# New assumed costs, a due time one pair sooner and a fourth row buffer in the planner of an attention and MLP kernel

## The chip, the cores and the metric

The kernel runs on one core of a Trainium2 chip. The metric is the device time of one execution in microseconds (us), and the median of several runs is compared. The engines are called as in the profile: PE (TensorE matmul), PEld (its weight loads), DVE (VectorE), ACT (ScalarE), POOL (GpSimd) and SP (SyncE, which here issues all DMAs).

## The reference, cut to what matters

```python
# attention: q, k, v are (8, 8, 576, 64), float32
scores = np.matmul(q, k.transpose(0, 1, 3, 2)) / np.sqrt(64)
scores = np.where(block_i >= block_j, scores, -1e9)     # blocks of 64, causal by block
attn = np.exp(scores - scores.max(-1, keepdims=True))
attn = attn / (attn.sum(-1, keepdims=True) + 1e-09)
o = np.matmul(attn, v)                                  # heads joined: x is (8, 576, 512)
# layer norm and MLP with a residual
mu, var = mean(x), mean((x - mu) ** 2)
xn = (x - mu) / np.sqrt(var + 1e-06) * g_ln
return x + np.maximum(xn @ w_ch1, 0.0) @ w_ch2          # 512 -> 2048 -> 512
```

The weights come in as 64-bit numbers; the kernel decodes them to float32 itself.

## The kernel before, in words

**Work.** Attention goes over 32 pairs of heads (`pair(k)`). For a pair, PE makes scores (L416), DVE takes the row minimum of the negated scores while it masks them (`soften`, L434), ACT takes the exponential (L437), PE transposes (L446), ACT or DVE copies the transposed block out of PSUM (`evac`, L234 for ACT and L236 for DVE), PE multiplies with v (L452, L456), and DVE transposes the result (L530). On PE the transposes and products of pair k stand behind the scores of pair k + 1. Every eighth pair, `first(m)` handles the first 64 positions of eight pairs (L568 to L615 on PE, DVE, ACT and POOL).

The MLP handles 36 tiles of 128 rows in rounds of 8, 8, 8, 8 and 4 tiles. A round has 8 weight groups; each makes 7 products (L867, a one-level Strassen scheme on operands split into a high and a low part) and then the second matrix product (L927), whose results DVE adds up (L936). Before a round, `norm_tiles(n, q)` normalises its rows two tiles at a time (four calls in a round of eight; `x0` buffers in round 0, `x` buffers in later rounds), and `operands(n)` makes the sums, differences and high and low parts (`diff` L754, `split` L763 and L765, tile `xm`). `decode(j, second)` decodes 32 pieces of the weights: ACT (L350, L355), POOL (L353, L373), DVE (L359, L362), and a cast on ACT or DVE. In round 0, `stream` turns decoded pieces into group operands (L818 loads `wf`, L826 sums on POOL, L837 low parts, L845 stores).

**Order.** The order of all instructions is written by a planner (`Plan.run`), which plays the program with assumed costs: `add(engine, cost, ...)` gives each task an assumed time, `any_of` lets the planner choose between engines by which would finish first, and a ready task with the lowest `prio` goes first on its engine. The order of instructions on each engine, and the engine of each `any_of` task, is then fixed; the chip runs each engine's list in that order, with waits. The assumed times change nothing else in the program.

**Priorities.** A pair k has `prio` 100 + 10 k and a little more at each step. So a task with `prio` 100 + 10 c stands behind the pairs before c and ahead of the pairs after c: it is a filler until pair c and overtakes from then on. `norm_tiles` of round 0 has c = 10 + 3 q + LATER, the operands of round 0 c = 22 + LATER, and decoding piece n has c = 12 + 0.97 n + LATER. `first(m)` has c = 8 m + 3. The MLP's own tasks have `prio` 0 to 4 for what follows a product. A task also has a gate, an earlier event that it waits for, which the change leaves alone. A rule in the planner (`AHEAD`) holds back a filler on DVE or ACT if a task of a pair at least half a pair more urgent will be ready before the filler's assumed end less 0.25 us.

**Buffers.** Tiles share pools: `small` has 21 tiles of 128x512, with a limit for each kind (`ya` 10, `x` 3, `t` 4, `tt` 4, `mag`, `sgn`, `xnt`, `x0`, `sum` 2 and others).

Of the kernel before, what the change touches and what calls it, by code (L numbers as in the profile page):

```python
# [9 lines left out]
F32 = mybir.dt.float32  # L10
# [8 lines left out]
P = 128  # L19
# [8 lines left out]
TILES = sum(ROUNDS)  # L28
D_0, D_1 = 12.0, .97
LN_0, LN_1 = 10, 3  # L30
LATER = 3
AHEAD = 100, 5, .25


# [155 lines left out]
def dve(n):  # L190
    return .07 + n / 960


def act(n, sbuf=False):
    return .055 + .085 * sbuf + n / 1200


def pool(n):
    return .07 + n / 440

@with_exitstack
def attn_mlp_kernel(ctx: ExitStack, tc: tile.TileContext, qk, qk0, v, v0, w1, w2, g, out):
# [8 lines left out]
    nc = tc.nc  # L211
# [16 lines left out]
    def any_of(fn, **costs):  # L228

        return {e: (c, lambda e=e: fn(engines[e])) for e, c in costs.items()}  # L230
# [51 lines left out]
    def small(name, shape, dtype, most):  # L282
        return kind(name, shape, dtype, 21, None, "small", most)
# [8 lines left out]
    new_ot, new_v0 = small("ot", [P, 512], F32, 2), small("v0", [P, 512], F32, 1)  # L292
    new_e0, new_pt00, new_ot0 = (small(n, [P, 512], F32, 1) for n in ("e0", "pt00", "ot0"))
    new_mag, new_sgn = (small(n, [P, 512], I32, 2) for n in ("mag", "sgn"))
    new_ya, new_x, new_xnt = (small(n, [P, 512], F32, k) for n, k in (("ya", 10), ("x", 3), ("xnt", 2)))
    new_x0, new_xn = small("x0", [P, 512], F32, 2), small("xn", [P, 512], F32, 1)
    new_t, new_tt, new_sum = small("t", [P, 512], F32, 4), small("tt", [P, 2, 2, P], F32, 4), small("sum", [P, 2, 256], F32, 2)
    xs = [kind(f"xm{p}", [P, max(ROUNDS) // 2, 2, 2, P], F32R, 1)() for p in range(7)]
# [37 lines left out]
    def decode(j, second, prio, gate):  # L336
# [6 lines left out]
        def dma():  # L343
# [12 lines left out]
            out=sgn(), in_=wv(0).bitcast(U32), func=AF.Copy, scale=2.0 ** -29 * (1 - 2.0 ** -9), bias=-0.499),  # L356
            r=[word], w=[sign], prio=prio)
        sign2 = Buf(parent=sgnb)
        add("DVE", dve(n), lambda: nc.vector.scalar_tensor_tensor(  # L359
            out=sgn(), in0=wv(1), scalar=-2147483648, in1=sgn(), op0=ALU.bitwise_and, op1=ALU.bitwise_or),  # L360
            r=[sign, word], w=[sign2], prio=prio)
        add("DVE", dve(n), lambda: nc.vector.scalar_tensor_tensor(  # L362
            out=sgn(), in0=mag(), scalar=3, in1=sgn(), op0=ALU.logical_shift_left, op1=ALU.bitwise_or),
            r=[sign2, mag2], w=[full], prio=prio)
        w = lambda: sgn().bitcast(F32)
# [180 lines left out]
    def first(m):  # L546
# [4 lines left out]
        def pr():  # L551
            step[0] += 1
            return prio + .05 * step[0]
# [31 lines left out]
        def total():  # L585
            nc.vector.tensor_reduce(out=nm.t, in_=ev(e.t), op=ALU.add, axis=AX.X)
            nc.vector.tensor_scalar_add(nm.t, nm.t, 1e-9)
            nc.vector.reciprocal(nm.t, nm.t)
        add("DVE", dve(512) + .4, total, r=[p, *d], w=[r1], prio=pr())
        add("POOL", pool(512), lambda: nc.gpsimd.tensor_mul(  # L590
            ev(e.t), ev(e.t), nm.t.unsqueeze(2).to_broadcast([P, 8, 64])), r=[p, r1], w=[pn], prio=pr())
        tr, pt, turned_ = new_tr(), new_pt00(), Buf()
# [49 lines left out]
    def norm_tiles(n, q, prio, gate):  # L642
# [74 lines left out]
        for h, (x, part) in enumerate(rows):  # L717
            unit, scaled = Buf(parent=x), Buf(parent=x)
            if n:
                add("ACT", act(512, True), lambda x=x, h=h: nc.scalar.activation(  # L720
                    out=x.t, in_=x.t, func=AF.Identity, bias=norm.t[:, 10 + h:11 + h], scale=norm.t[:, 4 + h:5 + h]),
                    r=[rstd], w=[unit, *part], prio=prio)
            else:
                add("DVE", dve(512), lambda x=x, h=h: nc.vector.tensor_scalar(  # L724
                    out=x.t, in0=x.t, scalar1=norm.t[:, 2 * h:2 * h + 1], scalar2=norm.t[:, 4 + h:5 + h],
                    op0=ALU.subtract, op1=ALU.mult), r=[rstd], w=[unit, *part], prio=prio)
            add(any_of(lambda e, x=x: e.tensor_mul(x.t, x.t, g_sb), POOL=pool(512)), r=[unit, gb], w=[scaled], prio=prio)
            xnt, xw = new_xnt(), new_xw()
            add("DVE", dve(512), lambda x=x, xnt=xnt: nc.vector.transpose(xnt.t, x.t), r=[scaled], w=[xnt], prio=prio)
            parts = []  # L730
            for g4 in range(4):
                parts.append(Buf(parent=xw))
                load(32 * 2048, lambda xw=xw, xnt=xnt, g4=g4: nc.sync.dma_start(
                    out=xw.t[:, 32 * g4:32 * g4 + 32].rearrange("(k r) q -> r k q", r=32),
                    in_=xnt.t[32 * g4:32 * g4 + 32].rearrange("p (k q) -> p k q", q=32)), r=[xnt], w=[parts[-1]], prio=prio)
            half = Buf(parent=xt)
            load(P * 2048, lambda xw=xw, h=h: nc.sync.dma_start(
                out=xt.t[:, h].rearrange("p (c q) -> p c q", q=P), in_=xw.t.rearrange("(c p) q -> p c q", p=P)),
                r=parts, w=[half], alloc=[xt], prio=prio)
            ready.append(half)  # L740
# [4 lines left out]
    def operands(n, prio):  # L745
# [5 lines left out]

        def diff(p, q, i, in0, in1, r, w):
            new = Buf(parent=tts[q])
            add(any_of(lambda e: e.tensor_sub(tmp(q, i), in0(), in1()), DVE=dve(256), POOL=pool(256)),  # L754
                r=r, w=[new, *w], prio=prio + .1 * p + .01 * q)
            return new

        def split(step, p, q, src, r):
            old = held.get((n - 1, p), [])
            hi, lo = Buf(parent=xs[p]), Buf(parent=xs[p])  # L760
            three = lambda x: x.rearrange("p (c n) -> p c n", c=2)
            pr = prio + .1 * step + .01 * q
            add(any_of(lambda e: copy(e, xs[p].t[:, q, 0], three(src())), ACT=act(256, True), DVE=.08 + 256 / 1920),  # L763
                r=r, w=[hi, *old], prio=pr)
            add(any_of(lambda e: e.tensor_sub(xs[p].t[:, q, 1], three(src()), xs[p].t[:, q, 0]),  # L765
                       DVE=dve(256), POOL=pool(256)), r=[hi, *r], w=[lo, *old], prio=pr)
            got.setdefault(p, []).extend((hi, lo))
            return hi, lo

# [242 lines left out]
```

## Time and profile before

| | us |
|---|---|
| median of 3 runs | 1050.07 |
| lowest and highest run | 1049.4, 1050.23 |
| the profiled execution's own time | 1050.46 |
| its span, first to last instruction | 1048.7 |
| PE busy in the span | 1037.1 |

The profile is of one execution. Busy time of PE has modelled ends, so that small waits inside a stretch of matmuls may count as busy; the starts of instructions are the better ruler. An instruction's time in the trace may overlap the one behind it on the same engine a little.

### The profile page before, as it was taken

To read this page: it belongs to the slowest core of one execution; us is meant where nothing else is said; L and a number is where in the kernel's file an instruction comes from. 1 tells how busy PE (TensorE), PEld (TensorE's weight loads), DVE (VectorE), ACT (ScalarE), POOL (GpSimd) and SP (SyncE) were. 2 spreads that over 40 slices of the span, in tenths; PEclk is the share of its full clock that TensorE was granted. 3 is DMA by queue.
4 is the path that set the end of the run, shared out by engine and by line. 5 is a ranking of instruction groups with operands and counts; after the bars stand their busy time and mean duration, and the time that the engine had idled before them with its cause. 6 is when DMAs were issued, how large, how long until landed. Compare 5 with 4: busy or idle time off the path is not lost.

```text
span 1048.7 us, 17977 instructions
## 1 busy us (share of the span) xinstructions
PE 1037.1 (99%) x6256; PEld 852.4 (81%) x6256; DVE 743.7 (71%) x1629; ACT 524.0 (50%) x1264; POOL 286.3 (27%) x468
## 2 busy tenths in 40 slices
PE   8999999999999999999999999999999999999998
PEld 7877777777878888888888888888888888888997
DVE  5778999989878878885656684665595555465544
ACT  6999888899875535342433341343242322122221
POOL 0223454545343765340222240222240220000000
PEclk9999999999999999999999999999999999999999
DMA  7578889898779898858777647688657667336873
GB/s 270 200 256 266 222 288 279 234 300 295 261 272 306 276 310 238 251 209 265 217 243 213 231 159 259 186 242 248 183 200 262 207 192 251 139 111 249 299 279 126
DMA packets 237930, 248.91 MB, mean 237 GB/s; under 512 B 159376, under 2 KB 188048, under 8 KB 227600
## 3 DMA queue, kind: packets, MB, share of 16 engines
q1 hardware_dynamic: 237840, 247.77, 72.9%
q8 instruction: 49, 0.80, 0.3%
q14 instruction: 41, 0.34, 0.1%
HBM read 182.71 MB, written 65.01 MB: 236 GB/s over the span
## 4 chain that ended last, share of the span: by engine, by line
PE 90%; DVE 7%; DMA 1%; issue 1%; ACT 0%; SPq 0%; POOL 0%; DVEq 0%; POOLq 0%; ACTq 0%
PE y L927 36%; PE p L867 32%; PE tr L446 7%; PE s L416 7%; PE o L456 5%; PE o L452 2%; DVE pab L434 1%; DMA wc<-wcs 1%; DVE pu L434 1%; DMA x<-xd 1%; DVE sgn L359 0%; DVE x L724 0%; DVE ya L936 0%; DVE xm L765 0%; PE tr L326 0%
## 5 line engine op out<-in xcount | busy, mean ns | idle before, releaser
L927 PE MATMUL y<-wc,h 128*128 128x512 f32 x1728 | 433.8, 390 | 0.2 <-DVE h L887 0.2
L927 PEld LDWEIGHTS y<-wc,h 128*128 128x128 f32 x1728 | 322.1, 188 | 66.4 <-DVE h L887 1.3
L936 DVE TENSOR_TENSOR ya<-y,ya 128x512 f32<-128x512 f32 x288 | 197.6, 687 | 181.6 <-PE y L927 178.8
L867 PE MATMUL p<-xm,wa 128*128 128x512 f32 (+1 forms) x960 | 221.7, 368 | 0.0
L867 PEld LDWEIGHTS p<-xm,wa 128*128 128x128 f32 x960 | 169.9, 188 | 31.5 <-issue 0.2
L867 PE MATMUL p<-xm,wb 128*128 128x512 f32 (+1 forms) x720 | 166.2, 368 | 0.0
L875 ACT COPY t<-p 128x512 f32<-128x512 f32 (+1 forms) x120 | 65.2, 544 | 167.8 <-PE p L867 166.0
L867 PEld LDWEIGHTS p<-xm,wb 128*128 128x128 f32 x720 | 127.7, 188 | 23.7
L886 ACT ACTIVATE h<-t 128x512 fp32r<-128x512 f32 (+1 forms) x120 | 62.2, 579 | 162.5 <-DVE t L880 162.3
L880 DVE TENSOR_TENSOR t<-p,t 128x512 f32<-128x512 f32 (+1 forms) x120 | 76.3, 636 | 47.9 <-PE p L867 43.2
L416 PE MATMUL s<-raw 64*128 64x224 f32 (+3 forms) x768 | 97.2, 388 | 2.5 <-DVE nm L434 2.0
L437 ACT ACTIVATE pab<-pab,nm 128x448 f32<-128x448 f32 (+1 forms) x128 | 91.2, 731 | 0.2 <-DVE nm L434 0.2
L234 ACT COPY pt<-tr 128x512 f32<-128x512 f32 x166 | 87.0, 597 | 7.2 <-PE tr L446 5.8
L416 PEld LDWEIGHTS s<-raw 64*128 64x128 f32 x768 | 74.8, 188 | 18.8 <-issue 5.1
L434 DVE CUSTOM_DVE_ANT_0 pab<-s,never 128x448 f32<-128x448 f32 (+1 forms) x128 | 82.7, 684 | 2.2 <-PE s L416 1.8
L456 PE MATMUL o<-pt,v 128*64 128x256 f32 (+1 forms) x768 | 80.1, 344 | 0.0
L456 PEld LDWEIGHTS o<-pt,v 128*64 128x64 f32 x768 | 55.3, 137 | 27.6
L887 DVE SCALAR_TENSOR_TENSOR h<-t,h 128x512 fp32r<-128x512 f32 (+1 forms) x120 | 74.1, 666 | 3.9 <-ACT h L886 3.8
L353 POOL TENSOR_SCALAR mag<-mag 128x512 f32<-128x512 f32 x32 | 48.7, 1525 | 101.4 <-ACT mag L350 92.4
L681 POOL TENSOR_SCALAR norm<-norm 128x1 f32<-128x1 f32 x28 | 6.9, 245 | 248.5 <-ACT xn L678 248.5
L437 ACT ACTIVATE pu<-pu,nm 128x320 f32<-128x320 f32 (+1 forms) x128 | 64.8, 510 | 19.5 <-DVE nm L434 18.5
L446 PE MATMUL tr<-ident,pab 128*128 128x128 f32 x512 | 63.3, 274 | 3.9 <-DVE nm L434 2.8
(96 smaller groups left out, 1036.3 us busy)
## 6 DMA issues: line engine op xcount, KB each, us to landing
wc<-wcs SPq DMA_DIRECT2D x40, 1024.0 KB, 7.0
wa<-was SPq DMA_DIRECT2D x32, 1024.0 KB, 6.3
wb<-wbs SPq DMA_DIRECT2D x32, 768.0 KB, 5.8
raw<-qk SPq DMA_DIRECT2D x32, 576.0 KB, 4.8
wr<-w SPq DMA_DIRECT2D x32, 512.0 KB, 6.1
v<-v SPq DMA_DIRECT2D x32, 320.0 KB, 5.5
x<-xd SPq DMA_DIRECT2D x144, 64.0 KB, 3.9
xrow<-x SPq DMA_DIRECT2D x36, 256.0 KB, 3.9
```

The source lines that it names most:

```text
L234: e.copy(out=out, in_=in_)
L416: nc.tensor.matmul(x, raw.t[HALF[h], 0, col], raw.t[HALF[h], 1, at:at + x.shape[1]], start=True, stop=True)
L434: add("DVE", dve(n) + .01, lambda: nc.vector.tensor_tensor_reduce(out=two(p.t[:, part(i, h)]), in0=mine(), in1=two(hide), scale=-0.125, sc ...
L437: add("ACT", act(n, True) + .14, lambda: nc.scalar.activation(out=p.t[:, part(i, h)], in_=p.t[:, part(i, h)], func=AF.Exp, bias=nm.t[:, at ...
L446: nc.tensor.transpose(o.t[:, n * P:(n + 1) * P], x, ident)
L456: nc.tensor.matmul(o.t[HALF[h], at + lo:at + 256], v_sb.t[:, ck, HALF[h]], rhs(h), start=False, stop=(n == len(steps) - 1), skip_group_che ...
L867: nc.tensor.matmul(x.t[:, 0:TN], w_(l), xs[m].t[:, 0:half, o, k], start=start and k == e == 0, stop=k == 1 and e == 2, skip_group_check=True)
L875: add("ACT", act(TN), lambda: nc.scalar.copy(out=t.t[:, 0:TN], in_=x.t[:, 0:TN]), r=[r], w=[new], prio=0)
L880: add("DVE", dve(TN), lambda: nc.vector.tensor_add(t.t[:, 0:TN], x.t[:, 0:TN], t.t[:, 0:TN]), r=r, w=[new], prio=0)
L887: add("DVE", dve(TN), lambda: nc.vector.scalar_tensor_tensor(out=x.t[:, 1, 0:TN], in0=src(), scalar=0.0, in1=x.t[:, 0, 0:TN], op0=ALU.max, ...
L927: nc.tensor.matmul(yb.t, x.t[:, l, at:at + P], wc.t[:, i, o], start=i == e == 0, stop=i == 1 and e == 2)
L936: add("DVE", dve(512), lambda yb=yb, ya=ya: nc.vector.tensor_add(ya.t, yb.t, ya.t), r=[part, before_], w=[now], prio=1)
```

## The change

Assumed times of some tasks become longer: two DVE instructions of decoding and one of normalisation (`dve2`), the differences and low parts of `operands` on DVE (`dve2`), its casts on DVE (`cast`), all POOL tasks priced by `pool`, and the sum in `first` on DVE (0.4 us more). `LATER` goes from 3 to 2. The kind `x` (rows of rounds 1 to 4) may have four buffers of the pool `small`, which stays at 21.

```diff
-LATER = 3
+LATER = 2
 def pool(n):
-    return .07 + n / 440
+    return .1 + n / 390
+def dve2(n):
+    return .1 + n / 760
+def cast(n):
+    return .2 + n / 1400
...
-    new_ya, new_x, new_xnt = (... for n, k in (("ya", 10), ("x", 3), ("xnt", 2)))
+    new_ya, new_x, new_xnt = (... for n, k in (("ya", 10), ("x", 4), ("xnt", 2)))
...
-        add("DVE", dve(n), lambda: nc.vector.scalar_tensor_tensor(     # decode, L359 and L362
+        add("DVE", dve2(n), lambda: nc.vector.scalar_tensor_tensor(
...
-        add("DVE", dve(512) + .4, total, r=[p, *d], w=[r1], prio=pr())
+        add("DVE", dve(512) + .8, total, r=[p, *d], w=[r1], prio=pr())
...
-                add("DVE", dve(512), lambda x=x, h=h: nc.vector.tensor_scalar(   # norm_tiles, L724
+                add("DVE", dve2(512), lambda x=x, h=h: nc.vector.tensor_scalar(
...
-            add(any_of(... tensor_sub(tmp(q, i), ...), DVE=dve(256), POOL=pool(256)),     # diff, L754
+            add(any_of(... tensor_sub(tmp(q, i), ...), DVE=dve2(256), POOL=pool(256)),
...
-            add(any_of(... copy(e, xs[p].t[:, q, 0], ...), ACT=act(256, True), DVE=.08 + 256 / 1920),
+            add(any_of(... copy(e, xs[p].t[:, q, 0], ...), ACT=act(256, True), DVE=cast(256)),
...
-                       DVE=dve(256), POOL=pool(256)), r=[hi, *r], w=[lo, *old], prio=pr)   # L765
+                       DVE=dve2(256), POOL=pool(256)), r=[hi, *r], w=[lo, *old], prio=pr)
```

`dve(n)` is 0.07 + n / 960 and `act(256, True)` is 0.353. The assumed times in us, before and after: `dve` to `dve2` of 512 0.603 and 0.774, of 256 0.337 and 0.437; a cast of 256 on DVE 0.213 and 0.383; `pool` of 512 1.234 and 1.413, of 256 0.652 and 0.756.

## Rows read from the trace of the kernel before

**Rows 1.** The page of the profile: busy time, share of the span and instructions of each engine, and the busy tenths of PE in 40 slices.

```profile
PE 1037.1 (99%) x6256; PEld 852.4 (81%) x6256; DVE 743.7 (71%) x1629; ACT 524.0 (50%) x1264; POOL 286.3 (27%) x468
PE   8999999999999999999999999999999999999998
```

**Rows 2.** Busy time of each engine in stretches (us from the span's start: length, then busy time and instructions of PE, PEld, DVE, ACT and POOL, granted clock of PE as a share, DMA share, GB/s).

```profile
100.00:275.00 175.00, 170.08 (x1642) 133.43 (x1640) 161.61 (x479) 155.29 (x423) 84.10 (x118) 1.00 0.88 273
...
303.00:471.00 168.00, 167.82 (x758) 137.63 (x757) 139.43 (x236) 79.66 (x162) 86.21 (x123) 1.00 0.83 268
471.00:925.00 454.00, 454.00 (x2005) 376.05 (x2004) 276.63 (x481) 144.42 (x296) 85.80 (x197) 1.00 0.68 214
925.00:1049.00 124.00, 119.99 (x684) 105.05 (x682) 69.50 (x138) 29.68 (x75) 3.09 (x4) 1.00 0.61 225
```

**Rows 3.** PE in order of time (start, duration): the first scores of pair 2, the start of `first(0)`, the scores of pairs 7 and 8, and the transposes behind the last pair's scores, where the next scores would stand; between the first and the last of these rows lie 30 steps of one pair and four `first` blocks.

```profile
19.88 2.86 PE L416 MATMUL s<-raw 64*128 64x320 f32 x24
...
37.35 0.69 PE L568 MATMUL tr<-qk 64*64 64x64 f32 x32
...
65.90 2.86 PE L416 MATMUL s<-raw 64*128 64x320 f32 x24
...
74.64 2.86 PE L416 MATMUL s<-raw 64*128 64x320 f32 x24
...
300.20 1.09 PE L446 MATMUL tr<-ident,pu 128*128 128x128 f32 x8
```

**Rows 4.** Waits of PE in the stretch from 100 to 275 us, all that the view lists: who was waited for, us in total, times, longest.

```profile
PE tr L446 <- DVE nm L434: 2.8, 3, 1.6
PE s L416 <- DVE nm L434: 0.9, 1, 0.9
PE tr L446 <- ACT pt L234: 0.6, 2, 0.3
PE s L416 <- DVE ot L530: 0.3, 1, 0.3
PE s L416 <- DVE sums_all L539: 0.2, 1, 0.2
```

**Rows 5.** Groups of DVE instructions from 100 to 275 us, those whose assumed time changes: count, busy us, mean ns of one, idle before.

```profile
L359 DVE SCALAR_TENSOR_TENSOR sgn<-wr,sgn 128x512 int32<-128x512 int32 x12 | 9.7, 812 | 0.0
L362 DVE SCALAR_TENSOR_TENSOR sgn<-mag,sgn 128x512 int32<-128x512 int32 x12 | 8.6, 715 | 0.3
L724 DVE TENSOR_SCALAR x<-x,norm 128x512 f32<-128x512 f32 x8 | 6.1, 773 | 0.0
...
L236 DVE CAST xm<-tt 128x256 fp32r<-128x256 f32 x12 | 5.1, 429 | 0.0
...
L236 DVE CAST xm<-xt 128x256 fp32r<-128x256 f32 x12 | 3.6, 332 | 0.0
L765 DVE TENSOR_TENSOR xm<-xt,xm 128x256 fp32r<-128x256 f32 x5 | 3.0, 625 | 0.0
L765 DVE TENSOR_TENSOR xm<-tt,xm 128x256 fp32r<-128x256 f32 x6 | 2.4, 403 | 0.0
```

**Rows 6.** The group of ACT in the same stretch that makes the same casts.

```profile
L234 ACT CAST xm<-tt 128x256 fp32r<-128x256 f32 x4 | 1.5, 412 | 1.1 <-POOL tt L754 1.1
```

**Rows 7.** DVE in order of time (start, duration): a decoding instruction at 108.86 and one at 163.57, a cast at 183.07, then the first, the second and a later instruction of a run of DVE that begins at 184.67, and the softmax step behind that run.

```profile
108.86 1.76 DVE L359 SCALAR_TENSOR_TENSOR sgn<-wr,sgn 128x512 int32<-128x512 int32 x1
...
163.57 0.69 DVE L359 SCALAR_TENSOR_TENSOR sgn<-wr,sgn 128x512 int32<-128x512 int32 x1
...
183.07 0.29 DVE L236 CAST xm<-tt 128x256 fp32r<-128x256 f32 x1
...
184.67 0.72 DVE L530 STREAM_TRANSPOSE ot<-o 128x512 f32<-128x512 f32 x1 [0.85 <-PE o L456]
185.31 0.51 DVE L724 TENSOR_SCALAR x<-x,norm 128x512 f32<-128x512 f32 x1
...
187.06 0.98 DVE L724 TENSOR_SCALAR x<-x,norm 128x512 f32<-128x512 f32 x1
...
191.06 0.45 DVE L434 CUSTOM_DVE_ANT_0 pu<-s,never 128x320 f32<-128x320 f32 x1
```

**Rows 8.** PE in order of time beside that run: the scores of pair 20, the transposes behind them, which waited, and the scores of pair 21.

```profile
185.18 3.12 PE L416 MATMUL s<-raw 64*128 64x320 f32 x24
...
191.86 1.53 PE L446 MATMUL tr<-ident,pab 128*128 128x128 f32 x12 [1.65 <-DVE nm L434]
...
196.50 2.86 PE L416 MATMUL s<-raw 64*128 64x320 f32 x24
```

**Rows 9.** POOL in order of time beside the decoding instruction at 108.86.

```profile
108.57 3.19 POOL L727 TENSOR_TENSOR x<-x,g_sb 128x512 f32<-128x512 f32 x2 [1.59 <-DVE x L724]
```

**Rows 10.** The queue of SP in order of time: the last store of a decoded first weight, the last load of such a weight by `stream`, and the last store of group operands.

```profile
374.62 1.08 SPq L378 DMA_DIRECT2D w1f<-sgn  x1
...
399.55 0.91 SPq L818 DMA_DIRECT2D wf<-w1f  x1
...
443.55 0.33 SPq L845 DMA_DIRECT2D wbs<-wb  x1
```

**Rows 11.** The page's DMA issues: the load of a pair's queries and keys, size and median us to landing.

```profile
raw<-qk SPq DMA_DIRECT2D x32, 576.0 KB, 4.8
```

More of the change, by code (lines that the diff above doesn't have):

```diff
@@ L294, in attn_mlp_kernel @@
     new_mag, new_sgn = (small(n, [P, 512], I32, 2) for n in ("mag", "sgn"))
-    new_ya, new_x, new_xnt = (small(n, [P, 512], F32, k) for n, k in (("ya", 10), ("x", 3), ("xnt", 2)))
+    new_ya, new_x, new_xnt = (small(n, [P, 512], F32, k) for n, k in (("ya", 10), ("x", 4), ("xnt", 2)))
     new_x0, new_xn = small("x0", [P, 512], F32, 2), small("xn", [P, 512], F32, 1)
@@ L358, in decode @@
         sign2 = Buf(parent=sgnb)
-        add("DVE", dve(n), lambda: nc.vector.scalar_tensor_tensor(
+        add("DVE", dve2(n), lambda: nc.vector.scalar_tensor_tensor(
             out=sgn(), in0=wv(1), scalar=-2147483648, in1=sgn(), op0=ALU.bitwise_and, op1=ALU.bitwise_or),
             r=[sign, word], w=[sign2], prio=prio)
-        add("DVE", dve(n), lambda: nc.vector.scalar_tensor_tensor(
+        add("DVE", dve2(n), lambda: nc.vector.scalar_tensor_tensor(
             out=sgn(), in0=mag(), scalar=3, in1=sgn(), op0=ALU.logical_shift_left, op1=ALU.bitwise_or),
@@ L753, in diff @@
             new = Buf(parent=tts[q])
-            add(any_of(lambda e: e.tensor_sub(tmp(q, i), in0(), in1()), DVE=dve(256), POOL=pool(256)),
+            add(any_of(lambda e: e.tensor_sub(tmp(q, i), in0(), in1()), DVE=dve2(256), POOL=pool(256)),
                 r=r, w=[new, *w], prio=prio + .1 * p + .01 * q)
@@ L762, in split @@
             pr = prio + .1 * step + .01 * q
-            add(any_of(lambda e: copy(e, xs[p].t[:, q, 0], three(src())), ACT=act(256, True), DVE=.08 + 256 / 1920),
+            add(any_of(lambda e: copy(e, xs[p].t[:, q, 0], three(src())), ACT=act(256, True), DVE=cast(256)),
                 r=r, w=[hi, *old], prio=pr)
             add(any_of(lambda e: e.tensor_sub(xs[p].t[:, q, 1], three(src()), xs[p].t[:, q, 0]),
-                       DVE=dve(256), POOL=pool(256)), r=[hi, *r], w=[lo, *old], prio=pr)
+                       DVE=dve2(256), POOL=pool(256)), r=[hi, *r], w=[lo, *old], prio=pr)
             got.setdefault(p, []).extend((hi, lo))
```

## The prediction

> **What bounds the kernel now.** I read the busy shares first [rows 1]. PE is busy nearly throughout, so a change that only reorders work can win no more than the time in which PE waits. The table by stretch says where that is [rows 2]. From 471 to 925 us PE is busy in every microsecond, and from 303 to 471 it misses 0.18 us. From 100 to 275 us it misses 4.9 us. The last stretch misses 4.0 us, mostly the end of the span behind the last product, where none of the edited work stands. What can be won lies in the attention stage.
>
> Busy time hides small waits, so I measured that stage by the starts of pairs [rows 3]. An undisturbed pair takes 74.64 - 65.90 = 8.74 us. The three pairs with the first `first` block take 65.90 - 37.35 = 28.55 us, that is 2.33 us above three plain pairs. From 19.88 to 300.20 us there are 30 pairs and four such blocks: 30 x 8.74 + 4 x 2.33 = 271.5 us are needed, 280.3 us pass, and **8.8 us** are lost. The waits of PE there name DVE for nearly all of what shows as idle, and no DMA [rows 4]. DVE is busy 161.6 of 175 us and ACT 155.3 [rows 2]: both are close to full, and work that is not urgent (decoding, normalisation, operands) sits in their lists between the softmax steps.
>
> **The change part by part.**
>
> *DVE's assumed times.* In the stretch from 100 to 275 us I compare means with what the planner assumed before [rows 5]. Decoding: 12 x (0.812 - 0.603) + 12 x (0.715 - 0.603) = 3.9 us. L724: 8 x (0.773 - 0.603) = 1.4. Casts: 12 x (0.429 - 0.213) + 12 x (0.332 - 0.213) = 4.0. Low parts: 5 x (0.625 - 0.337) + 6 x (0.403 - 0.337) = 1.8. Sum 11.1 us. But an instruction's time overlaps the next: the transpose at 184.67 lasts 0.72 us and the next starts after 0.64 [rows 7]. Taking 0.08 us off for each of the 67 instructions leaves **5.7 us** that the planner did not see on an engine that PE then waited for. The new prices add, for the same instructions, 32 x 0.170 + 11 x 0.100 + 24 x 0.170 = 10.6 us, and 0.4 us for each of three sums of `first`: 11.8 us. So the shortfall is covered about twice, and the planner will put less filler between softmax steps.
>
> What that is worth is bounded by 0 and by 8.8 us. Some of the loss isn't a matter of prices. From 184.67 to 191.06 DVE works through the L724 instructions, the steps of `first(2)` and two transposes before it takes pair 20's scores [rows 7]; PE waits 1.65 us, and pair 20 takes 11.32 us where a plain one takes 8.74 [rows 8]. I put 2.3 us on this. At the old prices these tasks sum to 6.3 us (five of 0.603, four of 0.337, one of 1.003, one of 0.89), against 6.4 measured. The planner saw it and ordered it, because this work outranks pair 20. That leaves 8.8 - 2.3 = 6.5 us. I take half of it, **3.2 us**: a full planner list moves filler out, but ACT, where a part must go, has little room, and the order between bursts is new throughout.
>
> *Casts.* At 0.213 DVE beat ACT's 0.353; at 0.383 ACT wins when both are free. DVE made 24 of the 28 casts of round 0, ACT 4 [rows 5, 6]. ACT's cast is measured at 0.412. If 12 move, DVE is relieved of 12 x 0.28 = 3.4 us (the bare cast, [rows 7]) and ACT gets 4.9 us, in a stretch where it has 19.7 us idle. It is part of the 3.2 us; without that room ACT's copies out of PSUM would be late instead, which PE waited for by 0.6 us [rows 4].
>
> *POOL's assumed times.* POOL is busy 84.1 of 175 us [rows 2]. Longer prices push `any_of` work towards DVE, against DVE's own new prices pushing the other way (256 elements: 0.437 and 0.756 now, 0.337 and 0.652 before; both differences are 0.32). I take 0; the ends are one low part more or less on DVE for each tile pair, 4 x 0.4 = 1.6 us either way.
>
> *One pair sooner.* A chain of `norm_tiles` overtakes pairs from 12, 15, 18 and 21 instead of 13, 16, 19 and 22; operands from 24. Its DVE steps, POOL's twelve small steps and two products by g, and the DMAs (8 row loads, 2 stores, 8 stores and 2 loads of the transposed rows per chain) move together, past pair loads in SP's queue and past decoding in POOL's. PE waited for no DMA there [rows 4], a pair's queries and keys are ranked two pairs ahead and land in 4.8 us [rows 11], so SP costs 0; if that cover went, one landing is the price. On DVE the move is a gain only if the chain ends earlier for something that waits, and nothing does before 303 us. Its loss is a further burst like that at 184.67, 2.3 us each. I take 0; ends 0 and three bursts, 6.9 us. For decoding the rank hardly matters below pair 31: pieces above n = 17 rank behind all pairs either way.
>
> *What the filler leaves behind.* If 11.8 us of assumed DVE time no longer fit, up to 11.8 / 1.55 = 7.6 pieces of decoding slide past 303 us; I take two. There DVE has 168 - 139.4 = 28.6 us idle [rows 2], 0.17 of the time, so a piece of 1.55 us delays the last one by about 9 us. The last decoded first weight is stored at 374.62 and its loader issues at 399.55 [rows 10]; with 5 us for the store to land, 20 us are free, or 2.2 pieces. So two pieces cost nothing; each further one up to 9 us.
>
> *A fourth row buffer.* It lets the rows of rounds 1 to 4 be fetched sooner. From 471 us PE never waits, so it can win nothing there; it takes one of the 21 `small` tiles that decoding (`mag`, `sgn`) and the MLP (`t`, `ya`) also need before 471, where PE lost 0.18 us with three. I take 0; its lower end is one displaced piece, within the 20 us.
>
> **Where a rule speaks against it.** The decoding instruction at 108.86 lasts 1.76 us while POOL runs two products [rows 9]; alone it lasts 0.69 [rows 7]. L724 shows 0.98 and 0.51 in the same way. So these instructions have two durations, and a mean fits neither. The Trainium skill, "SBUF — State Buffer", section "Who interferes with whom", says that a DVE instruction with two SBUF inputs, or a two-port one, and a GpSimd instruction reading SBUF exclude each other, the later one waiting for the whole of the earlier. These rows agree. By that rule no price cures the blocked part. Worked out from rows alone, the blocked part is 12 x (0.812 - 0.69) + 8 x (0.773 - 0.51) + 12 x (0.429 - 0.29) + 12 x (0.332 - 0.29) = 5.7 us, the whole shortfall: the waits would then only move.
>
> **The rivals.**
> A, the forecast: 1050.46 - 3.2 = 1047.3 for the profiled execution, which stood 0.4 us above the median, so 1046.9, say **1047.0**. Own range 1045 to 1049.
> B, waits only move: blocking and rank set them, not prices. 1050; own range 1048 to 1053. For it: the two durations, and the burst that was planned right. Against it: DVE is short by the repriced lines.
> C, slower: chains overtake a pair sooner and three of them (q = 1 to 3) make a new burst, 3 x 2.3 = 6.9 us, against the 3.2 gained: 1050.1 + 3.7 = 1053.8. It decides from two bursts on. For it: the burst at 184.67. Against it: a chain starts by its gate and its buffers, not by its rank.
> D, slower: three pieces slide, 27 us for 20 free, and PE waits 7 us in round 0's last group: 1054, and more with each piece. Against it: fillers had 13.4 us of DVE idle time.
> E, nearly the whole 8.8 us goes: 1042.
>
> **How the numbers follow.** About 0.2% (2.1 us) is what a measurement of this kernel can tell from no change. A 0.44 (0.40 faster, 0.04 same), E 0.06 (faster), B 0.25 (0.22 same, 0.03 slower), C 0.17, D 0.08 (both slower). Together faster 0.46, same 0.26, slower 0.28. The range runs from 1043 to 1054: it leaves out most of E, D and the tail of C, some 0.16.
>
> **What would show it.** Pair intervals from 19.88 on: the lost 8.8 us falls to about 5.6, with pair 20 still long. DVE busy from 100 to 275 us falls by several us, ACT's casts of `xm` rise from 4 towards 16, decoding's last L359 starts after 391 us, PE stays full from 303 to 925. A new wait of PE for `nm` near pairs 15, 18 or 21 shows C; one on L867 or L927 before 471 shows D. I am wrong if the pair intervals keep their sum.

## The result, and the profile after

The changed kernel takes **1063.56 us** (median of 4 runs, 1063.4 to 1065.87) where the kernel before takes 1049.85: a ratio of **1.0136**, 95% interval 1.0123 to 1.0148. It is 1.4% slower. The forecast was 1047.0, with a range up to 1054, so the result lies outside it. The span of the profiled execution grew from 1048.7 to 1061.6 us. In the changed kernel the lines below the new functions stand 9 lower (L867 is L876).

The page of the changed kernel, to be laid beside [rows 1]: busy time of the engines, and PE's busy tenths in 40 slices.

```profile
PE 1041.1 (98%) x6256; PEld 852.4 (80%) x6256; DVE 748.6 (71%) x1590; ACT 529.0 (50%) x1284; POOL 298.1 (28%) x487
PE   8999999999999889999999999999999999999998
```

PE's busy time grew by 4 us only, but two slices that were full show 8: a slice is 26.5 us, so they cover 345 to 398 us. That is the first round of the MLP, behind attention. The table by stretch says the same, columns as in [rows 2]:

```profile
100.00:275.00 175.00, 170.31 (x1635) 133.23 (x1632) 157.27 (x465) 155.82 (x428) 76.97 (x112) 1.00 0.84 259
303.00:471.00 168.00, 160.54 (x713) 130.56 (x712) 139.30 (x216) 80.76 (x164) 97.64 (x130) 0.98 0.88 280
471.00:925.00 454.00, 452.13 (x1989) 372.51 (x1988) 279.83 (x473) 146.43 (x307) 95.50 (x215) 1.00 0.68 216
```

From 100 to 275 us little changed. From 303 to 471 PE misses 7.5 us, where it missed 0.18 [rows 2]. The list of PE's waits from 303 us on is short (who was waited for, us in total, times, longest):

```profile
PE p L876 <- ACT t L884: 7.9, 2, 6.7
PE y L936 <- DVE h L896: 0.8, 3, 0.4
PE p L876 <- DVE t L889: 0.5, 1, 0.5
```

I split every kernel below at one point: the start of the first long stream of MLP products (12 matmuls in a row, 307.84 us before, 307.05 after). What lies ahead is called attention, what lies between it and PE's last matmul the MLP. In the two profiled executions attention became 0.8 us shorter, and **the MLP 13.7 us longer** (737.16 to 750.88).

**The largest single loss.** PE of the changed kernel in order of time, then ACT, SP's queue, and the chain that ended last, in the same stretch:

```profile
365.67 2.88 PE L936 MATMUL y<-wc,h 128*128 128x512 f32 x12
375.23 2.93 PE L876 MATMUL p<-xm,wb 128*128 128x512 f32 x6 [6.68 <-ACT t L884]
377.95 2.40 PE L936 MATMUL y<-wc,h 128*128 128x512 f32 x6
380.19 1.53 PE L876 MATMUL p<-xm,wa 128*128 128x512 f32 x6
```

```profile
363.67 0.68 ACT L364 ACTIVATE sgn<-wr 128x512 int32<-128x512 uint32 x1
374.59 0.59 ACT L884 COPY t<-p 128x512 f32<-128x512 f32 x1 [10.24 <-DMA xw<-xnt]
```

```profile
357.74 0.43 SPq L941 DMA_DIRECT2D ya<-xrow  x1
...
363.14 7.04 SPq L742 DMA_DIRECT2D xw<-xnt  x4
```

```profile
357.74 7.83 DMA ya<-xrow
365.57 0.02 issue
365.58 4.07 SPq L742
369.65 0.04 issue
369.70 4.71 DMA xw<-xnt
...
374.59 0.60 ACT t L884
375.18 0.04 issue
375.23 2.93 PE p L876 x6
```

PE waits 6.68 us for a copy of a product out of PSUM (`t`). The copy reads nothing from a DMA. It waits for four **stores** of a normalised, transposed row (`xw<-xnt`). `t` and `xnt` are kinds of the same pool `small`: this `t` has the tile that an `xnt` had before, and may not be written until the four stores of that `xnt` have left. SP had issued them late: its queue was held for 7.04 us, and the chain follows this back to a load that was on its way for 7.83 us. In the instruction list this copy waits for four transfers and PE:

```
L884 COPY t_4787<-p_4655 128x512 [waits DMAHW2_49,DMAHW1_49,DMAHW7_49,DMAHW0_49,PE_49]
```

The four transfers are the stores of `xnt_4716`, which had the tile before. Of the 120 copies `t` on ACT, 15 wait for four transfers in the changed kernel, 5 before; each of them has the tile of an `xnt`. That such stores hold SP's queue is not new. SP's queue of the kernel before, in the same place:

```profile
363.32 5.34 SPq L733 DMA_DIRECT2D xw<-xnt  x4
```

It was held 5.34 us there, and PE lost nothing: by the instruction list the next owner of that tile is a `sum` on POOL.

The wait costs more than its 6.68 us. Windows of the changed kernel, columns as in [rows 2] (granted clock third from the end):

```profile
362.50:375.00 12.50, 6.05 (x27) 4.69 (x25) 7.54 (x10) 2.26 (x5) 9.70 (x7) 0.92 1.00 325
375.00:378.00 3.00, 2.77 (x7) 2.19 (x8) 1.29 (x2) 2.12 (x6) 1.11 (x3) 0.50 1.04 319
378.00:381.00 3.00, 3.00 (x11) 2.40 (x10) 1.92 (x3) 0.00 (x0) 0.55 (x1) 0.70 1.06 323
```

Behind the idle time the granted clock is 0.50, the lower of TensorE's two levels, and 0.70 on average in the next 3 us. By the starts of the matmuls, twelve take 2.72 us at full speed and six 1.36; here 9.56, 2.72 and 2.24 us pass from one start to the next. In all the event cost 6.84 + 1.36 + 0.88 = 9.1 us of the 13.7.

### The profile page after: what moved, and what is told of

Same layout as the page of the kernel before. It is cut to its first block, busy times and chain, and to the rows that moved or that the text cites. A ratio compares the mean times of both kernels' runs of the same rounds, so it can differ in the third digit from the quotient of the medians.

```text
span 1061.6 us, 17992 instructions
## 1 busy us (share of the span) xinstructions
PE 1041.1 (98%) x6256; PEld 852.4 (80%) x6256; DVE 748.6 (71%) x1590; ACT 529.0 (50%) x1284; POOL 298.1 (28%) x487
## 4 chain that ended last, share of the span: by engine, by line
PE 85%; DVE 8%; DMA 3%; issue 1%; ACT 1%; POOL 1%; SPq 0%; DVEq 0%; POOLq 0%; ACTq 0%
PE y L936 33%; PE p L876 28%; PE s L425 8%; PE tr L455 7%; PE o L465 6%; PE o L461 3%; DVE h L896 1%; DMA xrow<-x 1%; DVE ya L945 1%; DMA ya<-xrow 1%; DMA xt<-xw 1%; DVE xm L774 1%; DVE pab L443 1%; DMA xw<-xnt 1%; SPq L742 0%
## 5 line engine op out<-in xcount | busy, mean ns | idle before, releaser
L876 PE MATMUL p<-xm,wa 128*128 128x512 f32 (+1 forms) x960 | 221.2, 368 | 0.1
L876 PEld LDWEIGHTS p<-xm,wa 128*128 128x128 f32 x960 | 169.8, 188 | 32.0 <-ACT t L884 0.5
L876 PE MATMUL p<-xm,wb 128*128 128x512 f32 (+1 forms) x720 | 168.0, 371 | 8.4 <-ACT t L884 7.9
L876 PEld LDWEIGHTS p<-xm,wb 128*128 128x128 f32 x720 | 128.1, 189 | 34.1 <-ACT t L884 9.0
L446 ACT ACTIVATE pab<-pab,nm 128x576 f32<-128x576 f32 (+1 forms) x128 | 91.3, 732 | 3.4 <-DVE nm L443 3.3
L896 DVE SCALAR_TENSOR_TENSOR h<-t,h 128x512 fp32r<-128x512 f32 (+1 forms) x120 | 78.2, 702 | 7.1 <-ACT h L895 7.1
L455 PEld LDWEIGHTS tr<-ident,pab 128*128 128x128 f32 x512 | 56.5, 140 | 6.2 <-DVE pt L245 2.6
```

The lines of the kernel that those rows point to most:

```text
L446: add("ACT", act(n, True) + .14, lambda: nc.scalar.activation(out=p.t[:, part(i, h)], in_=p.t[:, part(i, h)], func=AF.Exp, bias=nm.t[:, at ...
L455: nc.tensor.transpose(o.t[:, n * P:(n + 1) * P], x, ident)
L876: nc.tensor.matmul(x.t[:, 0:TN], w_(l), xs[m].t[:, 0:half, o, k], start=start and k == e == 0, stop=k == 1 and e == 2, skip_group_check=True)
L896: add("DVE", dve(TN), lambda: nc.vector.scalar_tensor_tensor(out=x.t[:, 1, 0:TN], in0=src(), scalar=0.0, in1=x.t[:, 0, 0:TN], op0=ALU.max, ...
```

## The experiments

All times are in us. The ratio is taken against runs of the kernel before made beside each kernel (their medians lie between 1049.07 and 1049.85). The end of attention and the MLP part are those of one profiled execution, whose own time stands in the column "profiled". Some kernels scatter by 4 to 6.5 us between executions, and where the profiled execution lies at an end of that range (later_x4, costs_x4, xnt_apart20, decode_price), the two parts do not stand for the median.

The split point isn't quite the same work in all of them. Most kernels have one product of the MLP, six matmuls, ahead of it; costs_d6 and xnt_d10 have none there, xnt_rate80 has twelve matmuls. Six matmuls take 1.36 us. To be laid beside the others, costs_d6 has 741.0 in the MLP and 319.0 in attention, xnt_d10 744.8 and 306.6, xnt_rate80 740.8 and 309.8.

| kernel | median (lowest to highest) | ratio, 95% interval | profiled | attention | MLP |
|---|---|---|---|---|---|
| before | 1049.85 (1049.4 to 1050.23) | | 1050.46 | 307.84 | 737.16 |
| after | 1063.56 (1063.4 to 1065.87) | 1.0123 to 1.0148 | 1063.4 | 307.05 | 750.88 |
| x4_only | 1057.81 (1055.97 to 1058.24) | 1.0057 to 1.0087 | 1058.0 | 308.73 | 743.77 |
| x3_back | 1073.44 (1072.66 to 1074.73) | 1.021 to 1.0241 | 1074.73 | 307.96 | 761.31 |
| costs_only | 1054.62 (1053.46 to 1055.32) | 1.0029 to 1.0059 | 1054.67 | 304.77 | 744.42 |
| later_only | 1051.8 (1049.52 to 1052.85) | 1.0008 to 1.0027 | 1052.27 | 309.81 | 737.0 |
| later_x4 | 1060.68 (1057.59 to 1063.68) | 1.0074 to 1.0132 | 1057.59 | 308.94 | 743.19 |
| costs_x4 | 1054.29 (1052.5 to 1058.14) | 1.0036 to 1.008 | 1058.14 | 304.61 | 748.02 |
| xnt_apart20 | 1062.17 (1057.75 to 1064.29) | 1.01 to 1.0147 | 1057.75 | 307.82 | 744.46 |
| x4_xnt_apart | 1049.8 (1048.15 to 1050.94) | 0.9996 to 1.0015 | 1049.76 | 306.89 | 737.39 |
| decode_price | 1057.02 (1055.95 to 1061.06) | 1.0049 to 1.0101 | 1061.06 | 311.67 | 743.93 |
| costs_but_decode | 1060.01 (1059.27 to 1060.85) | 1.0079 to 1.0119 | 1059.27 | 314.54 | 739.27 |
| costs_d6 | 1065.35 (1063.96 to 1065.69) | 1.0138 to 1.0169 | 1065.5 | 317.66 | 742.37 |
| costs_skip | 1053.73 (1052.23 to 1055.95) | 1.0032 to 1.0072 | 1052.3 | 303.88 | 742.95 |
| costs_x4_xnt | 1053.38 (1051.07 to 1056.46) | 1.0025 to 1.0047 | 1052.88 | 304.61 | 742.78 |
| costs_hold | 1054.69 (1051.71 to 1055.62) | 1.002 to 1.0063 | 1054.69 | 305.12 | 744.12 |
| costs_x4_xnt_hold | 1053.06 (1051.22 to 1054.52) | 1.0015 to 1.0037 | 1053.96 | 305.59 | 742.91 |
| xnt_d10 | 1054.56 (1051.31 to 1057.73) | 1.0031 to 1.0066 | 1056.9 | 305.23 | 746.17 |
| xnt_rate80 | 1056.44 (1054.38 to 1057.49) | 1.0047 to 1.0077 | 1056.05 | 311.18 | 739.4 |
| xnt_skip | 1050.89 (1048.48 to 1054.25) | 1.0007 to 1.0032 | 1049.8 | 303.73 | 740.6 |

### The parts alone

**The fourth row buffer** in the kernel before (x4_only), and taken out of the changed one (x3_back):

```diff
-    ... (("ya", 10), ("x", 3), ("xnt", 2)))
+    ... (("ya", 10), ("x", 4), ("xnt", 2)))
```

> The kernel before with four row buffers and nothing else. Theory 1: the copies of products that wait for four transfers at once become more (16 in the instruction list, 5 with three buffers), and PE waits for ACT's copy for several us somewhere between 340 and 480 us: 1055 to 1064. Theory 2: no such wait, 1049 to 1051.

> The changed kernel with three row buffers again (x 3); prices and LATER stay. Theory 1 (the fourth row buffer makes the planner hand t, the MLP's copy of a product, a small tile whose former content, xnt, is still being stored, and PE waits for it): the 6.7 us wait of PE for ACT's copy at 368 us goes, and with it the low clock behind it, 9.3 us in all, and most of the 3.9 us of small losses after 425 us: 1049 to 1051. Theory 2 (new prices and the earlier due time move normalisation and decoding into the start of the MLP, and the wait is theirs): 1058 to 1064.

Measured: alone it adds 6.6 us to the MLP, and by medians 8.3 us to the time. Taken out of the changed kernel it does not bring the time back: the MLP grows by another 10.4 us. With three buffers 5 copies `t` wait for four transfers, as before the change, but the rows of round 1 now come late (the last is transposed at 469.5 us, before at 435.9), and PE stands between the rounds. Waits of PE in x3_back in order of time:

```profile
487.68 0.79 PE L876 MATMUL p<-xm,wa 128*128 128x512 f32 x1 [12.96 <-ACT xm L243]
492.78 6.23 PE L876 MATMUL p<-xm,wa 128*128 128x512 f32 x17 [4.31 <-DVE xm L774]
```

So in the changed order the fourth buffer prevents a loss at the end of round 0 and makes another in its middle.

**The prices alone** (costs_only: all new assumed times, `LATER` 3, three buffers), **one pair sooner alone** (later_only), and the two pairs with the fourth buffer (later_x4, costs_x4):

> The kernel before with the new prices alone (LATER 3, three row buffers). My prediction's term: attention shorter by 3.2 us, 1047. What the changed kernel's trace now makes likelier: attention shorter by 1 us or less, MLP as before, 1049 to 1051. If the prices alone disturb the MLP's start (theory 2): above 1053.

> The kernel before with LATER 2 alone. The runs with new prices differ in when attention ends: 304.8 us with LATER 3, 308.0 with LATER 2. If the earlier rank costs attention those 3.2 us by itself (overtaking), attention ends at 309 to 311 us and the MLP is as before: 1051 to 1053. If it costs only beside the new prices: 1049 to 1050.5.

> The kernel before with LATER 2 and four row buffers. If the parts add: 1057.8 (four buffers alone) plus what LATER 2 costs alone, 1057 to 1061. If the sum is set by how the parts fall together in the MLP's first round, it lies outside: below 1055 or above 1063.

> New prices and four row buffers, LATER 3: the changed kernel without the earlier rank. If the parts add, attention ends near 305.7 us (304.8 with the prices, 0.9 later with four buffers) and the MLP takes 737.2 + 7.3 + 6.6 = 751 us: 1062. If they hit the same room only once, the MLP takes 744 to 746: 1055 to 1058.

Measured: the prices shorten attention by 3.1 us and lengthen the MLP by 7.3. One pair sooner lengthens attention by 2.0 and leaves the MLP alone. later_x4 has the MLP of x4_only (743.19 and 743.77), and 15 copies waiting for four transfers; its profiled execution is the shortest of four. Prices and fourth buffer together add 10.9 us to the MLP in the longest of five executions of costs_x4. The three parts alone sum to 7.3 + 6.6 - 0.2 = 13.7, the whole, but that is chance, as the medians show.

**The parts do not add.** Each median less that of the kernel before beside it: fourth buffer 8.3, prices 5.1, one pair sooner 2.4; fourth buffer and one pair sooner 11.3, prices and fourth buffer 5.2, prices and one pair sooner 23.9 (x3_back), all three 13.7. So the fourth buffer costs 8 to 9 us at the old prices, nothing that shows beside the new ones, and in the changed kernel it saves 10. One pair sooner costs 2 to 3 us at the old prices, but 18.8 beside the new ones with three buffers and 8.5 with four. Of all steps this one, beside the prices, costs the most. What it does there was not traced, beyond the rows of round 1 that come late in x3_back.

### Is it the shared tile?

`xnt` gets two tiles of its own, and the pool shrinks by one; in the changed kernel (xnt_apart20) and in the kernel before with four row buffers (x4_xnt_apart):

```diff
-        return kind(name, shape, dtype, 21, None, "small", most)
+        return kind(name, shape, dtype, 20, None, "small", most)
-    new_ya, new_x, new_xnt = (small(n, ...) for n, k in ...)
+    new_ya, new_x, new_xnt = ((kind if n == "xnt" else small)(n, ...) for n, k in ...)
```

> The changed kernel, but xnt has two tiles of its own and the pool small has 20 instead of 21 tiles, so that t can never follow an xnt in a tile. Prices, LATER and four row buffers stay. Theory 1: no copy of a product waits for four transfers, PE's wait at 368 us goes: 1048 to 1051. Theory 2: the wait comes from the order and stays, 1058 to 1064.

> The kernel before with four row buffers, but xnt has two tiles of its own and the pool small has 20 tiles. No copy of a product waits for four transfers then (16 do with four row buffers alone, 5 in the kernel before). If these waits are what four row buffers cost, the MLP takes 737 to 739 us (743.8 with four row buffers alone): 1049 to 1052. If it is the larger number of rows under way at once (more work for DVE and ACT between 320 and 430 us), the MLP still takes 742 us or more: 1054 to 1059.

Measured: x4_xnt_apart has the MLP of before, 737.39 against 743.77 with the shared tile, and its time can't be told from before: the median is 1049.8, where x4_only has 1057.81. No copy `t` of it waits for four transfers, and its waits of PE from 303 us on are one line:

```profile
PE y L927 <- DVE h L887: 0.2, 1, 0.2
```

SP's queue still stands just as long on such stores there:

```profile
384.06 5.94 SPq L733 DMA_DIRECT2D xw<-xnt  x4
```

So at the old prices the cost of the fourth buffer is shown: it is who shares tiles with `xnt`. One rival was not run: `xnt` apart means 22 tiles in all in place of 21, and the tile more was not tried without the separation.

In the changed kernel the same edit removes the event: PE waits eight times in xnt_apart20, 1.1 us at most, and this is the largest group.

```profile
PE y L936 <- DVE h L896: 3.7, 6, 1.1
```

In that execution the MLP falls by 6.4 us, to what the prices alone leave (744.46 and 744.42). But it is the shortest of four: two of the others take 1064.2 us, as long as the changed kernel, and the medians, 1062.17 and 1063.56, can't be told apart. So the event is shown in the trace, and that the changed kernel would be faster without it is not shown. costs_x4_xnt below differs from xnt_apart20 by `LATER` 3 alone and stands 3.9 us above before, xnt_apart20 12.6: the rank costs its 8 to 9 us beside the prices without any tile shared with `xnt`, too.

In x4_only the largest loss, at 400 to 409 us, isn't a copy `t`. ACT stood 7.14 us before a row's statistics (`xn`), with a cast and the MLP's `h` behind them, and the trace names no releaser. The instruction list does: this `xn` is a kind of `small` too, has the tile of `xnt_4969`, and waits for that tile's four stores beside two loads of its row. The loads had been issued by 383.4 us; the last of the four stores was issued at 397.58, behind a queue that had been held. It is the same cause in another kind. SP and ACT of x4_only:

```profile
388.13 6.93 SPq L733 DMA_DIRECT2D xw<-xnt  x3
...
397.58 0.50 SPq L733 DMA_DIRECT2D xw<-xnt  x1
```

```profile
400.59 0.63 ACT L678 ACTIVATE xn<-x 128x512 f32<-128x512 f32 x1 [7.14 <-issue]
```

### Why do the prices cost 7 us in the MLP?

Where it is lost is clear: from 447.03 to 469.21 us PE starts 66 matmuls, which take 15.0 us at full speed, so 7.2 us are lost there. costs_only, PE, DVE and POOL in order of time:

```profile
449.76 2.55 PE L876 MATMUL p<-xm,wa 128*128 128x512 f32 x10 [0.41 <-DVE wa L846]
...
456.91 1.66 PE L876 MATMUL p<-xm,wb 128*128 128x512 f32 x6 [0.52 <-DVE t L889]
459.91 0.73 PE L936 MATMUL y<-wc,h 128*128 128x512 f32 x2 [1.34 <-ACT h L895]
462.01 0.96 PE L936 MATMUL y<-wc,h 128*128 128x512 f32 x3 [1.36 <-DVE h L896]
```

```profile
457.99 0.68 DVE L889 TENSOR_TENSOR t<-p,t 128x512 f32<-128x512 f32 x1
458.59 2.15 DVE L774 TENSOR_TENSOR xm<-xt,xm 128x256 fp32r<-128x256 f32 x3
460.67 2.42 DVE L896 SCALAR_TENSOR_TENSOR h<-t,h 128x512 fp32r<-128x512 f32 x3
...
463.62 0.74 DVE L774 TENSOR_TENSOR xm<-tt,xm 128x256 fp32r<-128x256 f32 x2
```

```profile
457.75 0.92 POOL L763 TENSOR_TENSOR tt<-xt 128x256 f32<-128x256 f32 x1
458.63 1.84 POOL L763 TENSOR_TENSOR tt<-xt,tt 128x256 f32<-128x256 f32 x2
461.54 1.01 POOL L774 TENSOR_TENSOR xm<-tt,xm 128x256 fp32r<-128x256 f32 x1 [1.07 <-ACT xm L243]
465.52 1.04 POOL L774 TENSOR_TENSOR xm<-xt,xm 128x256 fp32r<-128x256 f32 x1 [2.98 <-ACT xm L243]
```

Low parts of round 1's operands (L774) stand ahead of the MLP's `h` (L896) in DVE's list and take 0.72 us each beside POOL, against 0.37 at 463.62, where POOL stands idle. Windows of costs_only, then of before:

```profile
447.00:463.00 16.00, 12.29 (x48) 8.24 (x46) 16.00 (x28) 10.35 (x25) 11.03 (x13) 1.00 1.02 340
463.00:471.00 8.00, 7.85 (x27) 6.31 (x28) 7.45 (x17) 2.72 (x8) 2.53 (x3) 0.79 0.60 245
```

```profile
447.00:463.00 16.00, 16.00 (x72) 13.26 (x71) 16.00 (x34) 8.56 (x23) 10.10 (x10) 1.00 0.57 208
```

DVE is full for those 16 us in both kernels, and in before PE loses nothing. But before, DVE gets through 34 instructions in them, with costs_only through 28, with POOL and the DMA engines busier beside it; the mix of instructions differs too, so the count alone doesn't say why. What came so late is also to be seen in the lists: 24 of 32 decoding instructions of a kind stand ahead of the first product of the MLP on DVE before, 20 with the new prices; by their starts in the trace 22 and 19 lie ahead of 303 us. The last piece is decoded at 390.8 us before and at 427.0 in costs_only, and the weights of the last group are loaded at 399.6 and 437.

**Which price?** decode_price changes the two DVE instructions of decoding only; costs_but_decode changes all others:

> The kernel before with the new price for decoding's two DVE instructions alone. Theory 3 (the longer price of decoding lets fewer pieces into the attention stage; they slide into the MLP's first round, where the operands of its last groups and of the next round come late): 20 of 32 pieces stand ahead of the first sum of products in DVE's list, 24 in the kernel before; attention ends 1 to 3 us earlier, the last piece is decoded 30 us or more later, and the first round of the MLP loses 4 to 8 us: 1052 to 1056. Rival 4 (the casts that go to ACT, or POOL's prices, are what disturbs the MLP): 1048 to 1051.

> All new prices except that of decoding's two DVE instructions; LATER 3, three row buffers. Theory 3: 23 of 32 pieces stand ahead of the MLP as before, round 0 of the MLP loses at most 2 us and attention is 0 to 2 us shorter: 1047 to 1051. Rival 4: the MLP loses its 7 us here too, 1053 to 1056.

Measured: the MLP grows by 6.8 us with decoding's price and by 2.1 with the others. The number of pieces ahead of the MLP goes with it: 20 and 23 of 32. But attention becomes longer by 3.8 and by 6.7 us, where both together make it shorter by 3.1. The 3.8 are those of decode_price's longest execution, 4.0 us above its median, and may be its scatter; the four executions of costs_but_decode agree within 1.6 us. So the gain in attention isn't a sum of gains by price.

**Is it the displaced decoding?** costs_d6 has the prices and ranks decoding six pairs sooner (`D_0` 6 for 12); costs_skip has the prices and leaves out of the last four pieces their two DVE instructions (signs and low bits of those weights):

> The new prices alone, with decoding ranked six pairs sooner (D_0 6 instead of 12), so that 25 of 32 pieces stand ahead of the first sum of products in DVE's list (20 with the prices alone, 24 in the kernel before). Theory 3: the MLP takes 737 to 739 us again and attention pays for five more pieces, 5 x 1.4 = 7 us at most, 0 to 7 us: 1046.5 to 1053. If late decoding is not the cause, the MLP still takes 743 us or more.

> The kernel with the new prices alone, but the last four of the 32 pieces are decoded without their two DVE instructions (that part of the computation is left out): 4 x 2 x 0.69 = 5.5 us less on DVE, all of it late. Theory 3 (the late pieces overload DVE in the MLP's first round): from the end of attention to PE's end 737 to 740 us, where new prices alone take 744.4 and the kernel before takes 737.2; the time 1046 to 1050. If late decoding is not what costs it: still 743 us or more.

Measured: costs_d6 has 25 pieces ahead and, with the split point made the same, an MLP of 741.0: about half of the 7.3 us come back. The wait at 447 to 463 is gone, but a new one of 2.1 us for operands of round 1 stands at 484, and attention pays 11.2 us. costs_skip takes 1.5 us off the MLP, no more (its median stands 4.7 us above before, that of costs_only 5.1), and waits in the same place. Taken by itself DVE's load of late pieces explains little.

**Is it the operands of round 1, too late or badly placed?** costs_x4_xnt joins the prices with four row buffers and `xnt` apart, so that rows can come early; costs_hold holds the operands of rounds 1 to 4 back behind more urgent steps:

```diff
-        operands(n, 100 + 10 * (LN_0 + LN_1 * 4 + LATER) if n == 0 else 2)
+        operands(n, 100 + 10 * (LN_0 + LN_1 * 4 + LATER) if n == 0 else 110)
```

> The new prices and the fourth row buffer, LATER 3, with two tiles of their own for xnt and 20 tiles in small, so that no other tile waits for the four stores of an xnt. Theory 1, the ~7 us that the prices alone cost behind 303 us come from rows and operands of round 1 that are late: with rows that can be fetched earlier and no slot with pending stores the MLP's part takes 737 to 739 us, attention ends near 304.6, and the time is 1046 to 1048. Theory 2, they come from decoding and group sums that are late on DVE and POOL: the MLP's part stays at 743 to 745 and the time is 1053 to 1055. If neither, between, about 741.

> The prices alone, three row buffers, with one edit: the operands of rounds 1 to 4 get prio 110 in place of 2, so that the planner's rule for fillers holds them back from DVE and ACT where a more urgent step is about to be ready. Theory 1, operands of round 1 that stand ahead of t and h in DVE's list make PE wait: the MLP's part falls from 744.4 to 737 to 740 us. Theory 2, DVE and POOL have too much late decoding work in round 0: it stays at 743 or more. Attention is unchanged, near 304.8 us.

> Both edits: prices, four row buffers, xnt apart, and the operands of rounds 1 to 4 held back. If either theory of late or badly placed operands of round 1 holds, the MLP's part is 737 to 739 us and the time 1046 to 1048, which would be faster than both kernels; if decoding is the cause, 743 us and 1053.

Measured: 742.78, 744.12 and 742.91. In costs_x4_xnt the last row of round 1 is transposed at 417.8 us, 27 us sooner than in costs_only, and 5.6 us are still lost. costs_hold hardly changed what it was meant to: three L774 still stand ahead of `h` at 458 us. The planner holds a filler back only against its assumed times, in which L774 takes 0.437 us. So the placing of operands was not tested by it. Their lateness was, by costs_x4_xnt, and it is not the main cause: rows 27 us sooner bring back 1.6 of the 7.3 us.

**Decoding again, with early rows.** On top of costs_x4_xnt: decoding ranked two pairs sooner (xnt_d10), pieces due 0.80 pairs apart in place of 0.97 (xnt_rate80), and the DVE work of the last four pieces left out (xnt_skip, the same part as in costs_skip):

> As costs_x4_xnt (prices, four row buffers, xnt apart, 742.8 us of MLP), with decoding ranked two pairs sooner (D_0 10 in place of 12): in DVE's list 22 decoding instructions of a kind stand ahead of the MLP, where costs_x4_xnt has 20 and before 24. Theory, the pieces pushed behind 303 us cost the 5.4 us that are left: half of the lost pieces come back, the MLP's part falls to about 740, and attention grows by some 3 us at most: 1050 to 1053. If the count of pieces does not matter, the MLP's part stays at 743.

> As costs_x4_xnt, with decoding pieces due 0.80 pairs apart in place of 0.97 (D_1): 23 of 32 stand ahead of the MLP. By the theory of displaced pieces the MLP's part falls to 738 to 739; if attention then stays under 307 us the time is 1047 or less. If the count does not matter, 743.

> As costs_x4_xnt, with the last four pieces decoded without their two DVE instructions (left out: signs and low bits of those weights, so 5.5 us of DVE work less behind 303 us). Theory of late DVE work in round 0, now that rows are early: the MLP's part falls to 737 to 739 and the time to about 1047. If it stays at 742 or more, DVE's load is not what is missing, and the lateness of the last pieces lies in another part of their chain.

Measured: with 23 pieces ahead (xnt_rate80) the MLP falls to 739.4, but 1.4 us of that is the split point: laid beside costs_x4_xnt it is 740.8, above the 738 to 739 forecast, and attention grows by 5.2 us. With four pieces' DVE work gone it falls to 740.6. xnt_d10 missed: 22 pieces in the list, but only 20 started by 303 us, and a wait of 2.9 us for a copy `t` in a new place, at 405 us. What follows: with early rows, pieces left behind 303 us cost the MLP (2.0 to 2.2 us of 5.6 come back when they go), and pieces kept ahead of it cost attention more. The rest, about 3.5 us, wasn't traced to one cause. The DVE instructions made slower by POOL beside them are the best candidate, but a run that keeps POOL out of 447 to 463 us was not made.

No variant was faster than before.

## Why the prediction was wrong

**The prices' gain in attention: right in size.** The forecast took 3.2 us; costs_only gained 3.1. By the prediction's own ruler [rows 3] its stretch from pair 2 to the last transposes is 297.13 - 19.68 = 277.45 us, against 280.3 before. The rows of costs_only (PE in order of time):

```profile
19.68 2.86 PE L425 MATMUL s<-raw 64*128 64x320 f32 x24
...
297.13 1.09 PE L455 MATMUL tr<-ident,pu 128*128 128x128 f32 x8
```

That the size fits doesn't show the working, and the fit is in part luck: the prediction reasoned from prices that add up, and costs_but_decode goes the other way by 6.7 us. In the changed kernel the stretch takes 299.40 - 18.65 = 280.75 us, so the pair intervals kept their sum, which the prediction had named as its failure:

```profile
18.65 2.86 PE L425 MATMUL s<-raw 64*128 64x320 f32 x24
...
299.40 1.09 PE L455 MATMUL tr<-ident,pu 128*128 128x128 f32 x8
```

**Casts: right.** ACT makes 16 of the 28 casts from 100 to 275 us, as forecast. Groups of the changed kernel, to be laid beside [rows 5, 6]:

```profile
L243 ACT CAST xm<-tt 128x256 fp32r<-128x256 f32 x9 | 3.7, 413 | 0.5 <-POOL tt L763 0.3
L245 DVE CAST xm<-tt 128x256 fp32r<-128x256 f32 x7 | 2.4, 358 | 0.0
L243 ACT CAST xm<-xt 128x256 fp32r<-128x256 f32 x7 | 2.8, 413 | 0.0
L245 DVE CAST xm<-xt 128x256 fp32r<-128x256 f32 x5 | 2.3, 474 | 0.0
```

DVE's busy time there fell from 161.6 to 157.3 us, too. POOL's price alone was not tried.

**One pair sooner: taken as 0, measured 2.0 us of attention** (later_only), inside its bounds of 0 and 6.9 and a little under one burst. It is rival C in sign, below the two bursts at which C was to decide. Against the 3.1 us of the prices it leaves the 0.8 that the changed kernel shows in attention, near enough to 3.1 - 2.0. The larger part of its cost lies where the prediction looked for none: beside the new prices it adds 8.5 us or more to the time by medians, with three buffers mostly in the MLP (744.42 to 761.31), and the prediction priced it by attention alone.

**What the filler leaves behind: the mis-sized term.** The prediction let two of 7.6 pieces slide, 2.2 being free. Three slid (22 ahead of 303 us to 19), the last one started 36 us later with the prices alone (427.0 for 390.8) where 20 us were held to be free, and the prices alone cost the MLP 7.3 us in round 0's last group. That is rival D nearly to the word (three pieces, PE waits 7 us), given 8 in 100 because "fillers had 13.4 us of DVE idle time". The idle time of an average stretch was no room. By the planner's rule a filler must fit a gap between urgent steps, and a longer price fits fewer gaps; that is argued from the rule, the gaps were not counted. Its mechanism was too simple, though: D has PE wait for late weights, and the waits shown are mostly for `t` and `h`, made late by whatever was packed into the same 16 us. The sign named for D, a new wait on L867 or L927 before 471, came as well, but 6.7 us of it belong to the fourth buffer.

**The fourth row buffer: the step that failed.** The prediction saw that `small` is shared and took 0, with "one displaced piece" as the lower end; measured alone, it is 6.6 us of MLP and 8.3 us by medians, and in the changed kernel one event of 9 us. It counted tiles. What mattered is in what state a tile comes free: after an `xnt` it comes with stores in flight, and a copy or a row's statistics ahead of PE's next work waits for them. The row that could have warned is one that the prediction didn't look at, SP held 5.34 us by such stores at 363 us, on a stretch with a DMA share of 0.83 [rows 2]. "From 303 to 471 it misses 0.18 us" was read as room; it was a stretch that nothing happened to disturb, with DVE at 139 of 168 us.

**The sum of the parts: the second step that failed.** The forecast adds the parts, each priced alone. By the medians above they don't add: prices 5.1 and one pair sooner 2.4 make 23.9 together, and the fourth buffer then takes 10 off. The prediction had no term for this, and why prices and rank together cost so much stays open.

**PE full from 303 to 925 us: wrong**, and the table by stretch shows it at once. Of the 13.7 us, 9 are the event at 368 to 381; the rest are losses of a few tenths up to 1.4 us, over half of it between 425 and 477, where DVE is busy 49.6 of 52 us.

**The two durations: right, and more far-reaching than it was used.** The Trainium skill, "SBUF — State Buffer", section "Who interferes with whom", has DVE instructions with two SBUF inputs and GpSimd instructions that read SBUF exclude each other. The rows agree: L774 takes 0.72 us a piece with POOL at work beside it and 0.37 without. The prediction used it for rival B in attention only; the two durations lengthen the packed stretch of round 0 as well.

## What to carry to other kernels

When a pool is shared, ask of each kind what is still in flight when its tile comes free: kinds that leave by DMA should not hand their tiles to kinds on the critical path, and a bigger quota for one kind changes who inherits from whom. A stage with no idle time on its bound engine is not a stage with room; when fillers are displaced, price them where they land, with the queue and the shared ports as they are there. And new costs change a planner's whole order: here parts of 5 and 2 us made 24 together. So run each part alone and in pairs, and several times each; one profile of a kernel that scatters by 6 us doesn't price a part.

## What the hardware showed that was not expected

The clock took a share of several waits: after PE had stood 6.68 us the granted clock was 0.50 for 3 us and 0.70 on average in the next 3, and in costs_only, after waits of 1.34 and 1.36 us close together, 0.79 from 463 to 471 us. After a wait of 2.07 us in costs_d6 it was 0.68 from 484 to 488 us. But after xnt_d10's wait of 2.91 us, from 408 to 411 us, it stayed at 1.00. And SP's queue can stand for 5 to 7 us on four stores of `xnt` when the DMA share is near 1 (7.04 us in the changed kernel at 1.01, 5.34 before at 1.02), and the loads behind them are issued only then.
